# Layernorm, linear attention and a Mish feed-forward on one core: statistics by tile, the first weight matrix in three loads, the opening products on a constant, a new order of steps

## The chip, the core and the metric

The kernel runs on one core of a Trainium2 chip. The core has five engines with queues of their own: PE (TensorE, matrix products), ACT (ScalarE), DVE (VectorE), POOL (GpSimd) and SP (SyncE, which here only issues DMA transfers). Each engine takes its instructions strictly in the order in which they were written, and waits on semaphores for the other engines. The metric is the device time of one execution in microseconds; lower is better.

## What is computed

The reference, cut to what matters (`S` = 2048 rows, `D` = 448, 16 heads of 28, `F` = 1792; everything in bf16):

```python
def reference(A_x, A_wqkv, A_w_phi, A_wo, B_x, B_w1, B_b1, B_w2):
    xn = layernorm(A_x)                       # over the last axis, eps 1e-5
    q, k, v = split_heads(xn @ A_wqkv)
    pq, pk = q @ A_w_phi[h], k @ A_w_phi[h]   # per head, 28 x 28
    phi_q = concat(softmax(pq), softmax(-pq)) # 56 features
    phi_k = concat(softmax(pk), softmax(-pk))
    kv, z = phi_k.T @ v, phi_k.sum(rows)      # no causal mask
    o = (phi_q @ kv) / (phi_q @ z + 1e-6)
    h = xn @ B_w1 + B_b1
    act = h * tanh(softplus(h))               # Mish
    return A_x + o @ A_wo + act @ B_w2
```

## The kernel before

The 2048 rows are 16 tiles `t` of 128 rows, taken in 8 pairs `u`. All of it stays in SBUF. The steps are functions, each with a short name, and one long string `ORDER` (L147) lists the names in the order in which the functions are called (`run_order`, L163). Each function appends its operations to the queue of the engine that does them, so `ORDER` sets the order on every engine at once; `resolve` (L89) puts in the waits. A letter behind a name picks the engine: `a` for ACT, `d` for DVE, `p` for POOL, `m` or `s` for a transfer by SP, `b` for both ACT and DVE.

The stages, with the names that matter below:

- `z12` (`warm`, L366) puts 12 products of 128x128 by 128x512 ahead of everything on PE. Their operands are one element of a bf16 tile `zeros` that POOL clears (`zero`, L313), repeated by a stride of 0; nobody reads what they write.
- `lx0s` to `lx6s` load the rows of x, `lkms`, `lkts`, `lvms` the k and v parts of the qkv weights, `lqT0` to `lqT3` the q part transposed, `l1ms` and `l1ts` the matrix W1 (rows 0 to 383 in one load, the last 64 rows twice), `l2s` W2, `los` the output weights. All are issued by SP.
- `st` computes mean and variance of a pair (on DVE, or with `b` one of the two tiles on ACT), `rs` the power -1/2 of the variance (ACT: Ln and Exp; POOL: an add and a power), `xn` the normalised rows, `xt` their transposes (on PE with a copy out by ACT or DVE, or by a DMA transpose).
- `wtk`, `wmk`, `wmq` fold the 28x28 feature weights into the k and q weights (transposes and small products on PE, copies on ACT and DVE).
- `k`, `q`, `v` with a pair number are the projections of a pair, `f0.` and `f1.` the products with W1 for one of 14 column blocks and one half of the rows. Each has two parts: `F` is the three full chunks of 128 in the contraction (6 products), `H` the last 64 rows (2 products). The part that comes second closes the pair of PSUM banks and is followed by the copy out: two exponentials on ACT for k and q, one copy for v, one Mish activation on ACT for f.
- `kn` normalises phi_k (a sum and a reciprocal on DVE, a product on POOL), `kv` sums phi_k.T v on PE, `kvz` copies it out and has it transposed by DMA. `e` is the DMA transpose of phi_q of one tile. `nd` is the numerator and denominator of one tile on PE and the division on DVE, `ot` the DMA transpose of the result.
- `wo` and `g` (14 products a tile) are the products with the output weights and W2 into the same banks; `sto` and `stt` store. For the last tile, 15, the last 64 columns are computed apart (`last_columns`, L788).

A step that reads W1 waits for all of its loads, since `rows_of("W1")` (L287) lists them all, whichever rows the step needs.

Of the kernel before, what the change touches and what calls it, by code (L numbers as in the profile page):

```python
# [12 lines left out]
D = 448  # L13
# [3 lines left out]
P = 128  # L17
# [132 lines left out]
st4 k2F rs4p wmq0d xn4d xn5p wmq1a k3F v1Fd st0 q3F k1H q3H lx6s st6 v1Hd q2H q2F rs6p st7 k1F q1F rs0p xt4m xt5m  # L150
xn6d k4F rs7p k4H e6 v5Hd xn0d xt6m xn7d kn4.1 q1H k5H xt0m v5Fd k5F kn5.0 v6Fd kn5.1 k6F k0H xt7m ep e7 v6Ha k7H
l1ts l1ms k6H k7F kn6.0 k0F kn6.1 e3 q6F e2 v0Fa kn2.1 kn7.1 v4Fd v0Ha v4Hd kn4.0 q6H v7Hd kn3.0 v7Fa q4F e4 e12
f1.2H q4H e9 f0.2H kn2.0 e13 f0.2F kn7.0 f0.0F f1.2F f0.1F f0.0H f0.1H f1.3H q5H kn1.0 f1.3F kn0.1 e8 q0F q0H f0.3H
kn0.0 q7H kn3.1 e5 e1 q5F q7F f0.3F f1.7F kv7 kn1.1 kv0 kv4 kv6 kv3 kv2 kv1 e0 kv5 e10 f1.1H kvz f1.7H f1.8H f1.1F
f1.8F f0.6F e14 e11 f1.5H f0.6H nd2 f0.10F f1.5F nd1 f0.10H f0.5H f0.5F f1.11F nd3 ot1m f1.11H nd0 f0.13H f0.13F e15
f1.12F f1.0F f1.0H ot0m f1.12H los wob nd6 f1.13F f0.7F f1.10H f0.7H nd7 l2s ot3m f1.13H f1.10F f0.4F f0.4H nd5
f0.12H f0.9H f0.9F f0.12F nd4 f0.11H f0.8H f0.8F f0.11F f1.4F f1.6H f1.4H nd10 ot2m f1.9H f1.9F f1.6F wo3F wo3H nd11
nd13 nd12 ot5m ot6m g7 g6 g10 g11 wo5H nd15 nd14 wo2H wo5F ot7m g5 sto3 g4 wo2F wo6F sto5 wo6H wo1H nd9 nd8 wo1F sto2
g12 g2 g14 g13 wo7F wo0F ot4m wo0H sto6 wo4H wo7H g3 g0 wo4F g1 g8 stt14 sto0 g9 sto1 sto4 g15 stt15
"""  # L160
# [7 lines left out]
def _kernel(es, nc, A_x, A_wqkv, A_w_phi, A_wo, B_w1, B_b1, B_w2, out):  # L168
    def sb(name, shape, dtype):
        return es.enter_context(nc.sbuf_tensor(name, shape, dtype))  # L170
# [61 lines left out]
    def Eq_of(u):  # L232
        if u % 3 == 0:
# [5 lines left out]
                 "Wp1": [("Wp", 1, h, c) for h in range(2) for c in range(2)]}  # L239

    def oT_of(u):
# [6 lines left out]
    def bank(b, n=1):  # L248
        return PS[:, b * TCW:(b + n) * TCW]
# [61 lines left out]


    def p_zero():  # L313
        op("POOL", lambda e: e.memset(zeros[:], 0.0), w=[("zeros",)], tag="zeros")

# [50 lines left out]
    def warm(n):  # L366
        b = take1()

        def f(e):
            for _ in range(n):  # L370
                ins = e.matmul(bank(b)[:, :], ap_on(zeros[:, 0:1], [[0, P]]), ap_on(zeros[:, 0:1], [[0, TCW]]), start=True,
                               stop=True)
            return ins
        pe(f, [("zeros",)], [pb(b)], f"warm{n}")

# [66 lines left out]

    def ln_stats(u, both=False):
        for t in (2 * u, 2 * u + 1):
            if both and t % 2:
                i = u % 2
                op("ACT", lambda e, t=t: e.activation(junk[i][:], x_all[:, t, :], ACT.Copy, scale=1.0 / D,
                                                      accum_out=mv[:, t, 0:1]),
                   r=[("x", t), ("junk", i)], w=[("mean", t), ("junk", i)], tag=f"sm{t}")
                op("ACT", lambda e, t=t: e.mul(rmean[:, i:i + 1], mv[:, t, 0:1], D ** -0.5), r=[("mean", t)],  # L450
                   w=[("rmean", i)], tag=f"rm{t}")
                op("ACT", lambda e, t=t: e.activation(junk[i][:], x_all[:, t, :], ACT.Square, bias=rmean[:, i:i + 1],
                                                      scale=-D ** -0.5, accum_out=mv[:, t, 1:2]),
                   r=[("x", t), ("rmean", i), ("junk", i)], w=[("mv", t), ("junk", i)], tag=f"sq{t}")
                continue
            op("DVE", lambda e, t=t: e.bn_stats(stats[:, t, :], x_all[:, t, :]), r=[("x", t)], w=[("st", t)],  # L456
               tag=f"bn{t}")
            op("DVE", lambda e, t=t: e.bn_aggr(mv[:, t, :], stats[:, t, :]), r=[("st", t)], w=[("mv", t), ("mean", t)],
               tag=f"ag{t}")

    def ln_rstd(u, eng):
        a, b = 2 * u, 2 * u + 2
        if eng == "POOL":
            op("POOL", lambda e: e.tensor_scalar(lnv[:, a:b], mv[:, a:b, 1], float(LN_EPS), 0.0, op0=ALU.add,
                                                 op1=ALU.add),
               r=[("mv", a), ("mv", a + 1)], w=[("lnv", u)], tag=f"vare{u}")
            op("POOL", lambda e: e.tensor_tensor(rstd[:, a:b], lnv[:, a:b], mhalf[:], ALU.pow),
               r=[("lnv", u), ("eps",)], w=[("rstd", u)], tag=f"rstd{u}")
            return
        op("ACT", lambda e: e.activation(lnv[:, a:b], mv[:, a:b, 1], ACT.Ln, bias=eps_col[:]),  # L470
           r=[("eps",), ("table",), ("mv", a), ("mv", a + 1)], w=[("lnv", u)], tag=f"ln{u}")
        op("ACT", lambda e: e.activation(rstd[:, a:b], lnv[:, a:b], ACT.Exp, scale=-0.5),
           r=[("lnv", u)], w=[("rstd", u)], tag=f"rstd{u}")

    def ln_pair(u, eng):
        X = xn[u % NXN]
        a, b = 2 * u, 2 * u + 2
        if eng == "POOL":
            op("DVE", lambda e: e.scalar_tensor_tensor(shift[:, a:b], mv[:, a:b, 0], -1.0, rstd[:, a:b], ALU.mult,
                                                       ALU.mult),  # L480
               r=[("mean", a), ("mean", a + 1), ("rstd", u)], w=[("sh", u)], tag=f"sh{u}")
        for t in (a, a + 1):
            parts = [(0, D, 0)] if t % 2 == 0 else [(384, D, D), (0, 384, D + 64)]
            for n, (lo, hi, at) in enumerate(parts):
                if eng == "POOL":
                    op("POOL", lambda e, t=t, lo=lo, hi=hi, at=at: e.tensor_scalar(
                        X[:, at:at + hi - lo], x_all[:, t, lo:hi], rstd[:, t:t + 1], shift[:, t:t + 1],
                        op0=ALU.mult, op1=ALU.add),
                       r=[("x", t), ("sh", u), ("rstd", u)], w=[("xn", u % NXN, t % 2, n)], tag=f"xn{t}.{n}")
                else:  # L490
                    op("DVE", lambda e, t=t, lo=lo, hi=hi, at=at: e.tensor_scalar(
                        X[:, at:at + hi - lo], x_all[:, t, lo:hi], mv[:, t, 0:1], rstd[:, t:t + 1],
                        op0=ALU.subtract, op1=ALU.mult),
                       r=[("x", t), ("mean", t), ("rstd", u)], w=[("xn", u % NXN, t % 2, n)], tag=f"xn{t}.{n}")

# [358 lines left out]
    for u in range(NU):  # L854
        add(f"st{u}", ln_stats, u)
        add(f"st{u}b", ln_stats, u, True)
        add(f"xt{u}b", xT, u, "both")
        for eng, c in (("ACT", "a"), ("POOL", "p")):
            add(f"rs{u}{c}", ln_rstd, u, eng)
# [34 lines left out]
    for eng, c in (("SP", "s"), ("ACT", "a")):  # L894
# [13 lines left out]
    add("qd", double_qT)  # L908
    for n, fn in (("pi", p_ident), ("pm", p_mask), ("pw", p_wbd), ("pv", p_ones), ("pk", p_mask2), ("pp", p_pads), ("zero", p_zero)):
        add(n, fn)  # L910
    for n in (1, 2, 4, 8, 12):
        add(f"z{n}", warm, n)
# [53 lines left out]
```

## Time and profile before

| | us |
|---|---|
| median of 3 runs | 156.11 (155.65 to 156.21) |
| span of the profiled execution, first to last instruction | 152.5 |
| busy: PE, DVE, ACT, POOL | 147.9, 101.2, 74.9, 39.9 |
| the 12 opening products on PE | 0.95 to 6.25 |
| first product on real data | 6.70 |

The profile follows one execution. It lists its span, 152.5 us, and no time of the whole of it, so the span stands beside the median of the other runs, 3.6 us below it; that difference lies ahead of the first instruction and behind the last. A row of the timeline has the start in us from the span's start, the time from the first start to the last end, the engine, the line of the kernel, the operation with out<-in, the tile it works on, and how many instructions are merged in the row. In square brackets stands the idle time ahead of it and what ended it. `PEld` is the weight load of a product, which overlaps with the product ahead of it. A product's row contains the time until its result has landed; products in a row start closer together than their durations say.

### The profile page before, as it was taken

Reading aid. Unit: us, or ns where it says so; the run is one execution under the profiler, and the core shown is the slowest. Engines: PE = TensorE matmul, PEld = TensorE weight load, DVE = VectorE, ACT = ScalarE, POOL = GpSimd, SP = SyncE. Lnnn points to the kernel's source line nnn. Section 1 sums busy time; section 2 is a strip of 40 time slices with the busy share of each in tenths; the row PEclk is TensorE's granted clock in tenths of the full one; section 3 lists DMA queues with packets and bytes.
Section 4 is the critical chain, followed back from the end, with each engine's and each line's share of the span. In section 5 each row is a group of like instructions: output and inputs, shape, how many; then the busy total and the mean of one; then the engine's idle time right before and its main releaser. Section 6 shows DMA issues by size and latency. Waiting matters only on the chain.

```text
span 152.5 us, 2888 instructions
## 1 busy us (share of the span) xinstructions
PE 147.9 (97%) x1181; PEld 72.7 (48%) x1181; DVE 101.2 (66%) x227; ACT 74.9 (49%) x91; POOL 39.9 (26%) x58
## 2 busy tenths in 40 slices
PE   7899999999998999999999999999999999999993
PEld 2365444454443466444444444555555555455552
DVE  1699997999999203198999847798695970311221
ACT  4888899898599996757459657100000000000000
POOL 7452552499999950000000000000000000000000
PEclk9999999999999999999999999999999999999999
DMA  5995576889969176830379941030206111110302
GB/s 130 274 238 97 175 136 127 177 236 257 189 141 192 24 160 55 135 71 0 64 149 302 338 75 25 4 62 6 54 0 195 50 34 26 60 34 0 120 0 90
DMA packets 39961, 17.17 MB, mean 113 GB/s; under 512 B 33932, under 2 KB 39180, under 8 KB 39948
## 3 DMA queue, kind: packets, MB, share of 16 engines
q1 hardware_dynamic: 39804, 16.89, 49.2%
q8 instruction: 9, 0.15, 0.4%
q10 hardware_dynamic: 144, 0.10, 0.2%
q14 instruction: 4, 0.03, 0.1%
HBM read 7.02 MB, written 1.84 MB: 58 GB/s over the span
## 4 chain that ended last, share of the span: by engine, by line
PE 82%; DMA 7%; ACT 6%; SPq 2%; DVE 0%; issue 0%; ACTq 0%
PE PS L426 40%; PE PS L816 28%; PE PS L832 7%; DMA EqT<-actT 4%; DMA Wkv<-in_A_wqkv_dram 3%; PE PS L716 3%; PE PS L642 2%; ACT actT L613 2%; ACT actT L693 1%; ACT actT L674 1%; PE PS L575 1%; ACT L693 1%; ACT v_all L504 1%; SPq L268 1%; SPq L682 1%; PE PS L551 0%
## 5 line engine op out<-in xcount | busy, mean ns | idle before, releaser
L426 PE MATMUL PS<-xnT,W 128*128 128x512 bf16 (+1 forms) x224 | 46.3, 379 | 0.0
L816 PE MATMUL PS<-W,actT 128*128 128x448 bf16 (+1 forms) x224 | 42.8, 351 | 0.0
L693 ACT ACTIVATE actT<-PS,b1T 128x1024 bf16<-128x1024 f32 x28 | 30.3, 1114 | 13.1 <-PE PS L426 13.0
L816 PEld LDWEIGHTS PS<-W,actT 128*128 128x128 bf16 x224 | 21.8, 98 | 20.2 <-issue 0.4
L426 PEld LDWEIGHTS PS<-xnT,W 128*128 128x128 bf16 (+1 forms) x224 | 17.6, 97 | 23.7 <-issue 5.1
L625 POOL TENSOR_TENSOR actT<-actT,rSk 128x896 bf16<-128x896 bf16 x16 | 26.6, 1701 | 4.4 <-DVE rSk L623 4.4
L781 DVE TENSOR_TENSOR x_all<-PS,x_all 128x448 bf16<-128x448 f32 (+1 forms) x16 | 9.6, 617 | 20.9 <-PE PS L816 17.7
L621 DVE TENSOR_REDUCE Sk<-actT 128x32 f32<-128x896 bf16 x16 | 16.7, 1042 | 0.9 <-ACT actT L613 0.9
L613 ACT ACTIVATE actT<-PS 128x896 bf16<-128x896 f32 x16 | 13.7, 940 | 0.4 <-PE PS L426 0.4
L426 PE MATMUL PS<-Wpq,xnT 128*128 128x448 bf16 (+1 forms) x64 | 12.9, 353 | 0.5 <-ACT actT L693 0.5
L426 PE MATMUL PS<-Wpk,xnT 128*128 128x448 bf16 (+1 forms) x64 | 12.7, 353 | 0.0
L426 PE MATMUL PS<-Wkv,xnT 128*128 128x448 bf16 (+1 forms) x64 | 12.6, 353 | 0.0
L731 DVE COPY Sq<-PS 128x16 f32<-128x16 f32 x32 | 4.0, 167 | 10.8 <-PE PS L716 10.8
L456 DVE BATCH_NORM_STATS2 stats<-x_all 128x6 f32<-128x448 bf16 x14 | 8.5, 605 | 3.4 <-DMA x_all<-in_A_x_dram 3.4
L739 DVE TENSOR_TENSOR v_all<-v_all 128x464 f32<-128x464 f32 x16 | 10.3, 642 | 0.6
L735 DVE TENSOR_TENSOR v_all<-PS,Sq 128x464 f32<-128x464 f32 x16 | 10.3, 641 | 0.5
L742 DVE TENSOR_TENSOR xn<-v_all,rden 128x448 bf16<-128x448 f32 x16 | 10.0, 625 | 0.6
L737 DVE TENSOR_TENSOR v_all<-PS,Sq 128x464 f32<-128x464 f32 x16 | 10.1, 629 | 0.0
L674 ACT ACTIVATE actT<-PS 128x896 bf16<-128x896 f32 x10 | 8.5, 932 | 1.7 <-DMA EqT<-actT 1.7
L426 PEld LDWEIGHTS PS<-Wpq,xnT 128*128 128x128 bf16 (+1 forms) x64 | 5.3, 97 | 6.5 <-issue 1.1
L426 PEld LDWEIGHTS PS<-Wpk,xnT 128*128 128x128 bf16 (+1 forms) x64 | 5.3, 97 | 6.1 <-issue 1.9
L426 PEld LDWEIGHTS PS<-Wkv,xnT 128*128 128x128 bf16 (+1 forms) x64 | 5.0, 97 | 5.7 <-issue 1.5
(86 smaller groups left out, 118.0 us busy)
## 6 DMA issues: line engine op xcount, KB each, us to landing
W<-in_B_w_dram SPq DMA_DIRECT2D x1, 1568.0 KB, 7.8
out_dram<-x_all SPq DMA_DIRECT2D x7, 224.0 KB, 2.2
W<-in_B_w_dram SPq DMA_DIRECT2D x1, 1344.0 KB, 9.0
x_all<-in_A_x_dram SPq DMA_DIRECT2D x4, 224.0 KB, 3.2
x_all<-in_A_x_dram SPq DMA_DIRECT2D x2, 448.0 KB, 4.6
Wkv<-in_A_wqkv_dram SPq DMA_DIRECT2D x2, 336.0 KB, 4.5
Wo<-in_A_wo_dram SPq DMA_DIRECT2D x2, 336.0 KB, 3.9
W<-in_B_w_dram SPq DMA_DIRECT2D x2, 224.0 KB, 3.6
```

What stands on the lines that cost most here:

```text
L426: ins = e.matmul(o, lhs(c, k), rhs(c, k), start=first and c in (0, 3), stop=not first and c in (2, 3))
L613: op("ACT", lambda e, s=s: e.activation(E_of(u)[:, s, :, :], two(b, D), ACT.Exp, scale=1.0 if s == 0 else -1.0), r=[pb(b), pb(b + 1)], w=[ ...
L621: op("DVE", lambda e: e.tensor_reduce(Sk[u][:, s, :], Eh(), AX.X, ALU.add), r=[("E", u, s)], w=[("Sk", u, s)], tag=f"Sk{u}.{s}")
L625: op("POOL", lambda e: e.tensor_tensor(Eh(), Eh(), ap_on(rSk[u][:, s, 0:1], [[1, 2 * H], [0, DH]]), ALU.mult), r=[("E", u, s), ("rSk", u, ...
L674: op("ACT", lambda e, s=s: e.activation(Eq_of(u)[:, :, s, :].rearrange("p i (h n) -> p i h n", n=64)[:, :, :, 0:QP], two(b, D).rearrange(" ...
L693: op("ACT", lambda e: e.activation(actT[:, fc, q * 1024:(q + 1) * 1024], bank(b, 2), ACT.Mish, bias=b1T[:, fc:fc + 1]), r=[("b1T",), pb(b) ...
L735: op("DVE", lambda e: e.tensor_tensor(tv(t1[i]), num(0), sx(1), ALU.mult), r=[pb(b), pb(b + 1), ("Sq", i, 1)], w=[("t1", i)], tag=f"ta{t}")
L737: op("DVE", lambda e: e.tensor_tensor(tv(t2), num(1), sx(0), ALU.mult), r=[pb(b), pb(b + 1), ("Sq", i, 0)], w=[("t2",)], tag=f"tb{t}")
L739: op("DVE", lambda e: e.tensor_tensor(t1[i], t1[i], t2, ALU.add), r=[("t1", i), ("t2",)], w=[("t1", i)], tag=f"tc{t}")
L742: op("DVE", lambda e: e.tensor_tensor(o_sb[(t // 2) % 2][:, t % 2, :].rearrange("p (h d) -> p h d", d=DH), t1[i][:, :, 0:DH], ap_on(rden[i ...
L816: ins = e.matmul(bank(b)[:, 0:width(t)], actT[:, fc, tok(t)], W2[:, fc, 0:width(t)], start=first and fc == 0, stop=last and fc == FC - 1)
L832: ins = e.matmul(bank(b)[:, 0:n], oT_of(u)[lo:hi, cc * P:(cc + 1) * P], Wo[lo:hi, cc, 0:n], start=first and c in (0, 3), stop=last and c i ...
```

## The change

Four things are changed.

1. `zeros` and the step that clears it are gone. `warm` reads one element of a constant 1.0 that the framework keeps in SBUF, and waits for nothing. The constant that `scalar_like` gives is the float32 one, so the products are of float32 operands; there are 10 of them (`z10`) in place of 12. In the compiled program a float32 product is two pairs of weight load and matmul, so PE's queue begins with 20 such pairs; a bf16 product is one.
2. `st` and the waits on powers go by tile: `st3d` is tile 3 on DVE, `st2a` tile 2 on ACT, and `rs1t` does Ln and Exp of each of the two tiles by itself.
3. W1's 384 rows are loaded in three parts (`l1m0s`, `l1m1s`, `l1m2s`), each at a place of its own; a step that reads W1 waits for all three and for the last rows.
4. All steps stand in a new order. Among others the pairs 1 and 3 of x come first in place of 2 and 3, and ffn products with W2 (`g`) begin while products with W1 still run. The home of a transposed output is claimed by whichever pair comes first (`homes_taken`).

The order on PE at the program's beginning, where the opening products stand; before:

```order
L371 MATMUL PS<-zeros 128x512 [waits done_POOL]
L371 MATMUL PS<-zeros 128x512 x11
L551 MATMUL PS<-ident,Wkv 112x128 [waits dma_2,done_POOL]
L551 MATMUL PS<-ident,Wkv 112x128 x7
L499 MATMUL PS<-ident,xn 128x128 [waits done_DVE]
L499 MATMUL PS<-ident,xn 128x128 x6
```

and now:

```order
L376 MATMUL PS<-const-float32-1.0 128x512 x10
L552 MATMUL PS<-ident,Wkv 112x128 [waits dma_2,done_POOL]
L552 MATMUL PS<-ident,Wkv 112x128 x7
L500 MATMUL PS<-ident,xn 128x128 [waits done_DVE]
L500 MATMUL PS<-ident,xn 128x128 x6
```

The wait for POOL ahead of the first product is gone, the operand is the float32 constant, and the first product on real data follows the tenth, waiting for the same load of the k weights (`dma_2`) as before.

SP's queue around the loads of W1 (`W`) and the transposes of phi_q (`EqT`); before:

```order
L511 DMA_TRANSPOSE xnT<-xn 128x7x128 [waits done_DVE] x3
L682 DMA_TRANSPOSE EqT<-Eq 128x8x128
L276 DMA W<-in_B_w_dram 64x1792 x2
L271 DMA W<-in_B_w_dram 128x3x1792
L682 DMA_TRANSPOSE EqT<-actT 128x8x128 [waits done_ACT]
L682 DMA_TRANSPOSE EqT<-actT 128x8x128 x2
L682 DMA_TRANSPOSE EqT<-Eq 128x8x128 [waits done_ACT]
```

and now:

```order
L281 DMA W<-in_B_w_dram 64x1792 x2
L277 DMA W<-in_B_w_dram 128x1792
L512 DMA_TRANSPOSE xnT<-xn 128x7x128 [waits done_DVE] x3
L683 DMA_TRANSPOSE EqT<-actT 128x8x128 [waits done_ACT]
L683 DMA_TRANSPOSE EqT<-actT 128x8x128
L683 DMA_TRANSPOSE EqT<-actT 128x8x128 [waits done_ACT]
L683 DMA_TRANSPOSE EqT<-Eq 128x8x128 [waits done_ACT]
L277 DMA W<-in_B_w_dram 128x1792
L512 DMA_TRANSPOSE xnT<-xn 128x7x128 [waits done_POOL]
L683 DMA_TRANSPOSE EqT<-Eq 128x8x128
L277 DMA W<-in_B_w_dram 128x1792
```

The one large load ahead of the next transposes of phi_q has become three smaller ones, the second behind four of these transposes and the third behind a fifth; a transpose of x (of pair 0, normalised by POOL) now stands between the two transposes of phi_q of pair 3.

The end of SP's queue; before:

```order
L846 DMA out_dram<-x_all 128x448 [waits done_DVE]
L846 DMA out_dram<-x_all 128x896 [waits done_DVE]
L846 DMA out_dram<-x_all 128x896
L846 DMA out_dram<-x_all 128x896 [waits done_DVE]
L843 DMA out_dram<-x_all 128x64 [waits done_DVE]
```

and now:

```order
L848 DMA out_dram<-x_all 128x448 [waits done_DVE]
L848 DMA out_dram<-x_all 128x896 [waits done_DVE] x2
L848 DMA out_dram<-x_all 128x896 x2
L845 DMA out_dram<-x_all 128x64 [waits done_DVE]
```

Four stores of pairs stand behind that of tile 14 in place of three.

The diff, cut to its core:

```diff
 ORDER = """
-table lx2s zero lx3s pv st2b pw lkms lps pi pm st3b rs3a lkts z12 pp lbs rs2p lx1s xn2d xn3d wtk0b xt2b wtk1b lvms
-lx4s lqT2 st1 bd pk lqT0 xt3a b1 wmk0b lqT1 rs1a wmk1a xn1d st5 rs5p v2Fd lqT3 v3Fa v3Ha k2H v2Ha k3H qd xt1m lx0s
...
+pv lx1s st3d table pi pw st2a lx3s z10 lkms st6d lps lkts lbs lvms st7d rs1t pp xn1d lx2s rs3a lqT0 xn3d wtk0a xt1d
+wtk1b lx0s pm xt3b bd wmk0a wmk1a st4d v3Fd st5d lx6s v1Ha lqT1 rs2t lqT2 xn2d v3Ha b1 st15d st14d lqT3 qd xt2m k3H
+lx4s k3F v1Fa k1F wmq1a st0d rs7p st12d wmq0a xn7p xt7m l1ts st1d l1m1s st13d pk rs6p st11d k2F k2H k1H st8d st9d v2Ha
+q1H st10d q1F xn6d rs0p v2Fd q2F q3F k7H rs4p rs5p xt6m q2H q3H xn4d xn5d kn2.1 v7Ha xt4m v7Fd kn3.0 k7F xn0p v6Fa
+xt5m e2 k4F k4H k6H e3 e5 v6Hd q4H k6F e7 l1m2s q4F kn7.1 kn6.1 v5Fd v4Fd q6H xt0m k5H v5Hd e6 l1m0s k5F kn4.1 q6F
...
+f1.5H nd13 g2 f1.4F f1.7H f1.4H sto0 ot6m nd10 f1.7F f1.9F wo1F g6 f1.9H ot5m f1.12H nd14 wo3H f1.12F wo3F g7 wo5F nd9
+wo5H nd15 nd8 g10 ot7m g8 g12 wo6F sto1 g11 g5 g9 wo7F ot4m g4 wo6H wo4H wo7H wo2H g14 sto5 wo2F stt14 g13 wo4F sto6
+sto4 sto2 g15 sto3 stt15
 """
...
-    zeros = sb("zeros", [P, 2], BF16)
...
+    def load_chunk(eng, name, dst, src, c):
+        dma(eng, lambda e: e.dma_start(dst[:, c, :], src[c * P:(c + 1) * P, :]), w=[(name, 0, c)], tag=f"ld{name}.{c}")
...
-        return [(name, 0), ("Wt", 0), ("Wt", 1)] if name in ("Wk", "Wv") else [(name, i) for i in range(3)]
+        if name in ("Wk", "Wv"):
+            return [(name, 0), ("Wt", 0), ("Wt", 1)]
+        return [("W1", 0, c) for c in range(3)] + [("W1", 1), ("W1", 2)]
...
-    def p_zero():
-        op("POOL", lambda e: e.memset(zeros[:], 0.0), w=[("zeros",)], tag="zeros")
...
     def warm(n):
         b = take1()
+        one = nc.const_aps.scalar_like(1.0, ident[:, 0:1])
 
         def f(e):
             for _ in range(n):
-                ins = e.matmul(bank(b)[:, :], ap_on(zeros[:, 0:1], [[0, P]]), ap_on(zeros[:, 0:1], [[0, TCW]]), start=True,
-                               stop=True)
+                ins = e.matmul(bank(b)[:, :], ap_on(one, [[0, P]]), ap_on(one, [[0, TCW]]), start=True, stop=True)
             return ins
-        pe(f, [("zeros",)], [pb(b)], f"warm{n}")
+        pe(f, [], [pb(b)], f"warm{n}")
...
-    def ln_stats(u, both=False):
-        for t in (2 * u, 2 * u + 1):
-            if both and t % 2:
...
+    def ln_stats(t, eng):
+        if eng == "ACT":
...
+        for n, m in ((a, b),) if eng == "ACT" else ((a, a + 1), (a + 1, b)):
+            op("ACT", lambda e, n=n, m=m: e.activation(lnv[:, n:m], mv[:, n:m, 1], ACT.Ln, bias=eps_col[:]),
+               r=[("eps",), ("table",)] + [("mv", t) for t in range(n, m)], w=[("lnv", t) for t in range(n, m)], tag=f"ln{n}")
+            op("ACT", lambda e, n=n, m=m: e.activation(rstd[:, n:m], lnv[:, n:m], ACT.Exp, scale=-0.5),
+               r=[("lnv", t) for t in range(n, m)], w=[("rstd", t) for t in range(n, m)], tag=f"rstd{n}")
...
-        home = [("oT", u)] + ([x for n in oT_home[u // 2][2] for x in home_rows[n]] if u % 2 == 0 else [])
+        home = [("oT", u)] + ([x for n in oT_home[u // 2][2] for x in home_rows[n]] if u // 2 not in homes_taken else [])
+        homes_taken.add(u // 2)
...
-        add(f"l1m{c}", load_main, eng, "W1", W1, B_w1)
+        for i in range(3):
+            add(f"l1m{i}{c}", load_chunk, eng, "W1", W1, B_w1, i)
...
-    for n in (1, 2, 4, 8, 12):
+    for n in (4, 8, 10, 12, 14):
         add(f"z{n}", warm, n)
```

More of the change, by code (lines that the diff above doesn't have):

```diff
@@ L153 @@
[L153 to L157, printed above, removed]
@@ L439, in step @@
         return add
[L443 to L459 removed]
+    def ln_stats(t, eng):
+        if eng == "ACT":
+            i = t // 2 % 2
+            op("ACT", lambda e: e.activation(junk[i][:], x_all[:, t, :], ACT.Copy, scale=1.0 / D, accum_out=mv[:, t, 0:1]),
+               r=[("x", t), ("junk", i)], w=[("mean", t), ("junk", i)], tag=f"sm{t}")
+            op("ACT", lambda e: e.mul(rmean[:, i:i + 1], mv[:, t, 0:1], D ** -0.5), r=[("mean", t)], w=[("rmean", i)],
+               tag=f"rm{t}")
+            op("ACT", lambda e: e.activation(junk[i][:], x_all[:, t, :], ACT.Square, bias=rmean[:, i:i + 1],
+                                             scale=-D ** -0.5, accum_out=mv[:, t, 1:2]),
+               r=[("x", t), ("rmean", i), ("junk", i)], w=[("mv", t), ("junk", i)], tag=f"sq{t}")
+            return
+        op("DVE", lambda e: e.bn_stats(stats[:, t, :], x_all[:, t, :]), r=[("x", t)], w=[("st", t)], tag=f"bn{t}")
+        op("DVE", lambda e: e.bn_aggr(mv[:, t, :], stats[:, t, :]), r=[("st", t)], w=[("mv", t), ("mean", t)], tag=f"ag{t}")
     def ln_rstd(u, eng):
@@ L465, in ln_rstd @@
                                                  op1=ALU.add),
-               r=[("mv", a), ("mv", a + 1)], w=[("lnv", u)], tag=f"vare{u}")
+               r=[("mv", a), ("mv", a + 1)], w=[("lnv", a), ("lnv", a + 1)], tag=f"vare{u}")
             op("POOL", lambda e: e.tensor_tensor(rstd[:, a:b], lnv[:, a:b], mhalf[:], ALU.pow),
-               r=[("lnv", u), ("eps",)], w=[("rstd", u)], tag=f"rstd{u}")
+               r=[("lnv", a), ("lnv", a + 1), ("eps",)], w=[("rstd", a), ("rstd", a + 1)], tag=f"rstd{u}")
             return
[L470 to L473, printed above, removed]
+        for n, m in ((a, b),) if eng == "ACT" else ((a, a + 1), (a + 1, b)):
[3 more added lines that the diff above has]
+               r=[("lnv", t) for t in range(n, m)], w=[("rstd", t) for t in range(n, m)], tag=f"rstd{n}")
     def ln_pair(u, eng):
@@ L854, in _kernel @@
     for u in range(NU):
-        add(f"st{u}", ln_stats, u)
-        add(f"st{u}b", ln_stats, u, True)
+        for t in (2 * u, 2 * u + 1):
+            for eng, c in (("DVE", "d"), ("ACT", "a")):
+                add(f"st{t}{c}", ln_stats, t, eng)
         add(f"xt{u}b", xT, u, "both")
-        for eng, c in (("ACT", "a"), ("POOL", "p")):
+        for eng, c in (("ACT", "a"), ("POOL", "p"), ("tiles", "t")):
             add(f"rs{u}{c}", ln_rstd, u, eng)
@@ L908, in _kernel @@
     add("qd", double_qT)
-    for n, fn in (("pi", p_ident), ("pm", p_mask), ("pw", p_wbd), ("pv", p_ones), ("pk", p_mask2), ("pp", p_pads), ("zero", p_zero)):
+    for n, fn in (("pi", p_ident), ("pm", p_mask), ("pw", p_wbd), ("pv", p_ones), ("pk", p_mask2), ("pp", p_pads)):
         add(n, fn)
-    for n in (1, 2, 4, 8, 12):
+    for n in (4, 8, 10, 12, 14):
         add(f"z{n}", warm, n)
```

17 lines of the change are left out of this document (9 added, 8 removed).

## Prediction

> **What bounds the kernel now.** I read the page's busy times first, then PE's waits, then PE in order of time, then the chain of waits.
>
> ```profile
> span 152.5 us, 2888 instructions
> PE 147.9 (97%) x1181; PEld 72.7 (48%) x1181; DVE 101.2 (66%) x227; ACT 74.9 (49%) x91; POOL 39.9 (26%) x58
> PE PS L371 <- POOL zeros L314: 1.0, 1, 1.0
> PE PS L551 <- DMA Wkv<-in_A_wqkv_dram: 0.7, 2, 0.4
> PE PS L426 <- ACT actT L693: 0.5, 1, 0.5
> ```
>
> PE is busy for 97% of the span, and its waits are three lines that add up to 2.2 us. In order of time they lie here:
>
> ```profile
> 0.95 5.30 PE L371 MATMUL PS<-zeros 128*128 128x512 bf16 x12 [0.95 <-POOL zeros L314]
> 6.70 0.63 PE L551 MATMUL PS<-ident,Wkv 128*112 128x128 bf16 x8 [0.45 <-DMA Wkv<-in_A_wqkv_dram]
> ...
> 7.97 0.65 PE L551 MATMUL PS<-ident,Wkv 128*112 128x128 bf16 x8 [0.23 <-DMA Wkv<-in_A_wqkv_dram]
> ...
> 46.90 0.36 PE L426 MATMUL PS<-Wpq,xnT 64*128 64x448 bf16 x2 [0.46 <-ACT actT L693]
> ...
> 149.45 0.57 PE L798 MATMUL PS<-W,actT 128*128 128x64 bf16 x14
> ```
>
> So the span is a sum over PE. Its opening products, which nobody reads, are busy from 0.95 to 6.25. Real work starts at 6.70, when the k weights have landed, and the last product ends at 150.02. Of the 147.9 us busy, 147.9 - 5.3 = 142.6 are real work; inside it PE idles 0.23 + 0.46 = 0.69, and 152.5 - 150.0 = 2.5 follow it. Whatever moves the start of real work moves the end, and nothing else has much to give: all idle time on PE between real work's start and its end is worth 0.69 us.
>
> **The change part by part.** The opening products first, since they stand ahead of everything on PE. PE's queue is in order, so the first product on real data cannot start before the tenth of them is done. Their start moves a little: the constants are written ahead of the kernel's own first steps, and the wait for `zeros` goes.
>
> ```profile
> 0.34 0.10 POOL L951 MEMSET const-float32-1.0<- 128x1 f32 x1
> ...
> 0.80 0.10 POOL L314 MEMSET zeros<- 128x2 bf16 x1 [0.29 <-POOLq L951]
> ```
>
> The other engines begin at 0.80, so I let PE begin there, 0.15 earlier. Then the price. Before, 12 products of bf16:
>
> ```profile
> L371 PE MATMUL PS<-zeros x12: 610/634/634, 1.0 to 5.6; 128*128 128x512 bf16 x12
> 52.71 2.75 PE L426 MATMUL PS<-xnT,W 128*128 128x512 bf16 x12
> PEclk9999999999999999999999999999999999999999
> ```
>
> The first row (durations least/median/most, first and last start) gives one start every (5.65 - 0.95)/11 = 0.427 us, and the second 2.75/12 = 0.23 us for products of the same width later on. PE starts slow, although the clock's row on the page, the third, shows full speed in every slice, and it is still slow in the twelfth product, at 5.65. The products of 128 columns at 6.70 are fast (8 in 0.63). I put the rise at 6.2.
>
> Now there are 10 products of float32, compiled to 20 pairs of weight load and product, each reading 4 bytes an element. No row of PE here has a 4-byte operand. The nearest rows are copies out of PSUM by other engines:
>
> ```profile
> 8.33 0.41 DVE L506 COPY Eq<-PS 112x512 bf16<-112x512 bf16 x1
> 10.85 0.62 DVE L506 CAST Wpk<-PS 128x448 bf16<-128x448 f32 x1
> 7.43 0.60 ACT L504 ACTIVATE Eq<-PS 112x512 bf16<-112x512 bf16 x1 [0.19 <-PE PS L551]
> 9.96 0.55 ACT L504 ACTIVATE Wpk<-PS 128x448 bf16<-128x448 f32 x1
> ```
>
> Per element a 4-byte source costs DVE (0.62/448)/(0.41/512) = 1.73 times a 2-byte one, and ACT (0.55/448)/(0.60/512) = 1.05 times. So a pair costs between once the bf16 row and twice it (twice the bytes). With the rise at 6.2, that is 5.4 us after the start:
>
> - once: 5.4/0.427 = 12.6 pairs slow, 7.4 at 0.23 = 1.7; real work starts at 0.8 + 5.4 + 1.7 = 7.9
> - 1.73 times: 5.4/0.739 = 7.3 slow, 12.7 at 0.40 = 5.1; at 11.3
> - twice: 5.4/0.854 = 6.3 slow, 13.7 at 0.46 = 6.3; at 12.5
> - twice and never fast: 20 at 0.854 = 17.1; at 17.9
>
> I take 1.73, from the engine that is nearer to a bound by bytes, inside the two ends. The cover is the wait for the k weights, which hides products up to 6.67 and no more; with real work at 11.3 some 4.6 us lie open.
>
> The Trainium skill, "FP8 and Floating Point Precision", section "TensorE Precision Notes", says that true FP32 takes four passes through the array. By it a product would cost 4 x 0.427 = 1.71 us slow and 0.92 fast, which is the line "twice"; no row here shows it.
>
> The statistics. One tile less goes through ACT and one more through DVE, and `rs1t` adds an Ln and an Exp of one column:
>
> ```profile
> 6.70 0.29 ACT L470 ACTIVATE lnv<-mv,eps_col 128x2 f32<-128x2 f32 x1
> 7.03 0.20 ACT L472 ACTIVATE rstd<-lnv 128x2 f32<-128x2 f32 x1
> ```
>
> That is 0.5 us on ACT, all ahead of 11.3 and under the opening products: 0. If the products were short, it would delay the first transposes by up to 0.5.
>
> W1 in three loads and the new order. The stall at 46.90 is the one thing that they can mend. The chain of waits tells where it comes from:
>
> ```profile
> 34.38 0.78 SPq L682
> ...
> 35.20 6.42 DMA EqT<-actT
> ACT actT L674 <- DMA EqT<-actT: 1.7, 1, 1.7
> EqT<-actT SPq DMA_TRANSPOSE x10, 3.3
> W<-in_B_w_dram SPq DMA_DIRECT2D x1, 1344.0 KB, 9.0
> ```
>
> A transpose of phi_q took 6.42 us where the median is 3.3, in the 9.0 us in which W1's large load was landing; ACT waited for it before it could overwrite phi_q's buffer, and PE ran out of PSUM banks 5 us later. With a third of the load at a time I expect this stall to go, -0.46, and the 0.23 at 7.97 too, since the tails of the weights have long landed by 11.3. But the new order brings a chain of its own. In SP's queue the second transpose of pair 3 stands behind a transpose of x that waits for POOL, and ACT's exponentials of pair 6 wait for it; and the operations on ACT leave little room:
>
> ```profile
> 20.61 1.30 PE L426 MATMUL PS<-Wpk,xnT 128*128 128x448 bf16 x6
> 21.74 1.30 PE L426 MATMUL PS<-Wpq,xnT 128*128 128x448 bf16 x6
> 19.25 1.73 ACT L674 ACTIVATE Eq<-PS 128x896 bf16<-128x896 f32 x2 [0.59 <-PE PS L426]
> ```
>
> A pair's k or q costs PE 1.13 for the full chunks and 0.19 for the rest, 1.32, against 1.73 on ACT. Summed in the written order, ACT's work is at most 0.5 us ahead of PE's before and 0.6 now, so four pairs of banks hold it as before. Two of v's copies move from ACT to DVE, which is busy for 66% of the span and waits for PE after them as it did. Bounds for stalls of the new order: 0 and 1.5, a transpose that lands 2.7 late of which ACT's slack takes 1.2 (before, ACT's 1.7 of waiting became 0.46 on PE). I take 0.3.
>
> The end. Four stores stand behind tile 14's in place of three, the last three behind tiles 8 and 9, some 1.0 us ahead of the end of the last products.
>
> ```profile
> 149.53 0.56 DVE x_all L781
> ...
> 150.31 0.33 SPq L843 DMA_DIRECT2D out_dram<-x_all  x1
> out_dram<-x_all SPq DMA_DIRECT2D x7, 224.0 KB, 2.2
> out_dram<-x_all SPq DMA_DIRECT2D x1, 16.0 KB, 1.7
> ```
>
> Three issues of about 0.5 end about when the last DVE operation does, and a store of 224 KB lands only 0.5 later than one of 16 KB, so the last small store is not held up: 0, at most +0.5.
>
> The sum for the span: 11.3 + 142.6 + 0.3 + 2.5 = 156.7, against 152.5, that is +4.2. The median of the runs is 3.6 above the profiled span; I carry that over: 160.3 us.
>
> **The rivals.** *The clock does not rise while the opening products run.* The trace shows it rise under bf16 products only; whether 4-byte ones, with pauses between columns, count for as much is not in it. At 1.73 they end at 0.8 + 20 x 0.739 = 15.6, at twice at 17.9, and real work then starts slow and, if it needs the same 5.4 us, loses half of them, 2.7. Span 15.6 + 2.7 + 142.6 + 0.3 + 2.5 = 163.7, or 166.0: 167.3 to 169.6 us. For it speaks that PE was slow for all of 5 us before; against it, that it was busy throughout, as it would be now. The Trainium skill, "TensorE: Matmul & The Clock Gate", Part 1, has the clock follow how busy PE was in a window of about 3.4 us that runs free; by that it rises under any products, the rise may fall earlier or later from one execution to the next, and the row agrees in so far as twelve starts from 0.95 to 5.65 were all slow.
>
> *The opening products cost little: the other side.* If each pair costs what a bf16 product does, real work starts at 7.9, and with both inner stalls gone and none of the new order the span is 7.9 + 142.6 + 2.5 = 153.0: 156.6 us, not slower by what can be told. The point from which it decides is real work's start at 7.4 (152.5 - 142.6 - 2.5), ten products in 6.6 us together: below it the change gains. At most it gains down to the wait for the k weights: 6.7 + 142.6 + 2.5 = 151.8, 155.4 us. For it: ACT's 1.05. Against it: twenty instructions in place of twelve, and twice the bytes.
>
> *The new order stalls on pair 3's transpose*, on top of the forecast: 3.2 late, 1.2 of it absorbed, 2.0 on PE: 162.0 us. For it: ACT has waited for just such a transfer. Against it: with PE 4.6 later, everything that does not hang on PE (loads, statistics, the transposes of x) is that much earlier beside it.
>
> *The change does not do what its words say.* That is so in one point: the constant is neither zero nor 2 bytes wide; the forecast is made of that. If the chip runs each of them as one bf16 product all the same, ten take 4.3, end by 5.1, and real work waits for the k weights at 6.70 as before: 6.7 + 142.6 + 0.3 + 2.5 = 152.1, 155.7 us.
>
> **How the numbers follow.** Forecast (rise during the products, a price between 1.4 and 2 times): 0.55. Clock not risen: 0.22. Stalls of the new order on top: 0.11. Little cost: 0.08. One pass: 0.04. The forecast's own range is 158.5 to 162.5: the line "twice" gives 12.5 + 142.6 + 0.3 + 2.5 + 3.6 = 161.5, and 1.4 times (9.0 pairs slow at 0.598, 11.0 at 0.32, real work at 9.7) gives 158.7. For 8 in 10 I take the forecast, the stalls and the half of the slow clock that lies at 1.73, and leave out the other side but for its edge: 157.5 to 168.5. A difference below 0.5%, 0.78 us, can't be told from none here. The last two cases lie between 155.4 and 156.6, mostly within 0.5%: 0.07 same, 0.03 faster, and 0.02 of them above, which joins the rest: slower 0.90.
>
> **What would show it.** The row of the opening products: 10 or 20 float32 products that end near 11 (right), by 7 (hidden), or beyond 15 with the first 128-column products of real work at half pace (clock). Real work's first row then starts without idle time ahead of it, in place of 0.45 on the k weights. PE's waits inside real work should add up to less than 0.7, without a line of ACT's Mish. The chain should run over PE from about 0.8 on. The forecast is wrong if real work starts before 8, if PE has more than 1.5 us of waits behind it, or if the span from PE's last product to the end grows beyond 3.

## The result, and the profile after

The changed kernel takes 159.52 us (median of 4 runs, 158.98 to 160.56) against 155.88 for the kernel before in the same runs: a ratio of 1.028, interval 1.020 to 1.036. The profiled execution took 159.65 us with a span of 157.9. Run once more in a later job the ratio was 1.032 (1.027 to 1.037), where 2.0 to 3.6% was expected. The forecast was 160.3. The kernel before took 154.5 to 154.6 us in the later jobs (medians of 17 to 23 runs), so its 155.88 here, a median of four, is on the long side and the ratio of 1.028 on the low one.

The page of the kernel after, its span, busy times and the row of the opening products (engine, operation, tile, count, then busy time, mean ns of one, idle time ahead):

```profile
span 157.9 us, 2913 instructions
PE 153.3 (97%) x1189; PEld 75.8 (48%) x1189; DVE 102.9 (65%) x226; ACT 73.6 (47%) x91; POOL 40.6 (26%) x58
L376 PE MATMUL PS<-const-float32-1.0 128*128 128x512 f32 x20 | 10.9, 708 | 0.8 <-PEq L955 0.8
```

PE is again busy for 97%, and the twenty float32 products make 10.9 us of that where twelve bf16 ones made 5.3. Without them PE's work is 153.3 - 10.9 = 142.4, as before (142.6). PE in order of time, every row with idle time ahead of it, and the first real products:

```profile
0.84 10.91 PE L376 MATMUL PS<-const-float32-1.0 128*128 128x512 f32 x20 [0.84 <-PEq L955]
11.58 0.61 PE L552 MATMUL PS<-ident,Wkv 128*112 128x128 bf16 x8
...
14.33 1.78 PE L430 MATMUL PS<-Wkv,xnT 128*128 128x448 bf16 x10
...
31.03 1.30 PE L430 MATMUL PS<-Wkv,xnT 128*128 128x448 bf16 x6 [0.32 <-DMA xnT<-xn]
32.75 1.78 PE L430 MATMUL PS<-Wpk,xnT 128*128 128x448 bf16 x10 [0.43 <-DMA xnT<-xn]
...
70.84 0.40 PE L717 MATMUL PS<-KVZ,EqT 56*128 56x60 bf16 x16 [0.36 <-DMA KVZ<-KVT]
...
154.73 0.57 PE L800 MATMUL PS<-W,actT 128*128 128x64 bf16 x14
```

Real work starts at 11.58 with no idle time ahead of it, 4.88 later than before. The two waits inside real work (0.23 on weights, 0.46 behind a Mish) are gone, and three others have come, 1.11 us together, all on DMA transposes: two of x (pairs 6 and 4), one of the summed phi_k v. The last product ends at 155.30 and 2.6 us follow. So the span grew by 4.88 at the start, 1.11 - 0.69 = 0.4 in the middle and 0.1 at the end, 5.4 in all.

How a float32 product is paid is read from its weight loads (start, duration, idle ahead):

```profile
3.53 0.34 PEld L376 LDWEIGHTS PS<-const-float32-1.0 128*128 128x128 f32 x1 [0.52 <-issue]
4.39 0.34 PEld L376 LDWEIGHTS PS<-const-float32-1.0 128*128 128x128 f32 x1 [0.52 <-issue]
5.12 0.19 PEld L376 LDWEIGHTS PS<-const-float32-1.0 128*128 128x128 f32 x1 [0.39 <-issue]
5.55 0.19 PEld L376 LDWEIGHTS PS<-const-float32-1.0 128*128 128x128 f32 x1 [0.24 <-issue]
5.98 0.19 PEld L376 LDWEIGHTS PS<-const-float32-1.0 128*128 128x128 f32 x1 [0.24 <-issue]
```

A pair of load and product takes 0.86 us at first and 0.43 from about 5.0 on: at the slow pace twice the 0.427 of a bf16 product, and at the fast pace about twice the 0.22 to 0.23 that bf16 products of this width take. The pace rose during these products.

### The profile page after: what moved, and what is told of

It reads as the page before. It is cut to its first block, busy times and chain, and to the rows that moved or that the text cites. A ratio compares the mean times of both kernels' runs of the same rounds, so it can differ in the third digit from the quotient of the medians.

```text
span 157.9 us, 2913 instructions
## 1 busy us (share of the span) xinstructions
PE 153.3 (97%) x1189; PEld 75.8 (48%) x1189; DVE 102.9 (65%) x226; ACT 73.6 (47%) x91; POOL 40.6 (26%) x58
## 4 chain that ended last, share of the span: by engine, by line
PE 81%; DMA 8%; DVE 4%; POOL 2%; ACT 2%; issue 1%; SPq 0%; DVEq 0%; ACTq 0%
PE PS L430 35%; PE PS L818 27%; PE PS L376 7%; PE PS L834 7%; DMA xnT<-xn 3%; DMA KVZ<-KVT 3%; PE PS L717 2%; DMA x_all<-in_A_x_dram 2%; PE PS L643 2%; POOL rstd L467 2%; DVE stats L458 1%; ACT Eq L505 1%; DVE KVT L655 1%; ACT Wpk L505 1%; DVE xn L492 1%
## 5 line engine op out<-in xcount | busy, mean ns | idle before, releaser
L430 PE MATMUL PS<-xnT,W 128*128 128x512 bf16 (+1 forms) x224 | 46.8, 379 | 0.0
L818 PE MATMUL PS<-W,actT 128*128 128x448 bf16 (+1 forms) x224 | 44.0, 351 | 0.0
L376 PE MATMUL PS<-const-float32-1.0 128*128 128x512 f32 x20 | 10.9, 708 | 0.8 <-PEq L955 0.8
L458 DVE BATCH_NORM_STATS2 stats<-x_all 128x6 f32<-128x448 bf16 x15 | 9.1, 605 | 3.6 <-DMA x_all<-in_A_x_dram 3.6
```

The lines of the kernel that those rows point to most:

```text
L376: ins = e.matmul(bank(b)[:, :], ap_on(one, [[0, P]]), ap_on(one, [[0, TCW]]), start=True, stop=True)
L430: ins = e.matmul(o, lhs(c, k), rhs(c, k), start=first and c in (0, 3), stop=not first and c in (2, 3))
L458: op("DVE", lambda e: e.bn_stats(stats[:, t, :], x_all[:, t, :]), r=[("x", t)], w=[("st", t)], tag=f"bn{t}")
L818: ins = e.matmul(bank(b)[:, 0:width(t)], actT[:, fc, tok(t)], W2[:, fc, 0:width(t)], start=first and fc == 0, stop=last and fc == FC - 1)
```

## Experiments

Each ratio is against the kernel before, run in the same job, with its 95% interval; its median there was 154.5 to 154.6 us.

| run | what it is | us | ratio |
|---|---|---|---|
| new_order_bf16 | changed kernel, ten bf16 opening products | 157.78 | 1.021 (1.018 to 1.024) |
| old_order_f32 | kernel before, ten float32 opening products | 158.63 | 1.026 (1.023 to 1.030) |
| old_order_bf16 | kernel before, twelve bf16 ones, constant 1.0 | 154.86 | 1.003 (1.000 to 1.006) |
| new_w1_whole | changed kernel, W1's rows in one load | 165.29 | 1.070 (1.065 to 1.076) |
| new_bf16_14 | changed kernel, fourteen bf16 opening products | 156.46 | 1.014 (1.011 to 1.017) |
| new_bf16_14_w1_late | the same, two loads of W1 later | 155.56 | 1.008 (1.005 to 1.012) |
| old_w1_three | kernel before, W1 in three loads | 153.92 | 0.996 (0.995 to 0.998) |
| old_bf16_10 | kernel before, ten bf16 opening products | 156.16 | 1.010 (1.005 to 1.015) |
| new_f32_6 | changed kernel, six float32 products | 158.05 | 1.023 (1.019 to 1.027) |
| changed_again | the changed kernel | 159.49 | 1.032 (1.027 to 1.037) |
| old_w1_three_14 | old_w1_three, fourteen opening products | 154.15 | 0.997 (0.995 to 1.000) |
| old_w1_three_b | old_w1_three, loads at other places | 155.53 | 1.007 (1.004 to 1.009) |

### The opening products undone, and alone

new_order_bf16:

```diff
-        one = nc.const_aps.scalar_like(1.0, ident[:, 0:1])
+        one = nc.const_aps.scalar_like(1.0, ident[:, 0:1], BF16)
```

> The changed kernel with one thing undone: the opening ten products read a bf16 constant 1.0 in place of the float32 one. Theory A (the opening products make the loss): they end near 5.1, real work starts at the landing of the k weights, 6.7, in place of 11.6, so the time falls by up to 4.9 us from 159.5, to 154.6; up to 1 us less if stalls that the late start hid come out, such as the waits for the transposes of x (0.75 us on PE in the changed kernel). Theory B (the new order makes the loss): real work starts at 6.7 but PE's waits grow by what was gained, and the time stays within 1 us of 159.5.

old_order_f32 (the kernel before with `warm` of the changed one, and `z10`):

```diff
+        one = nc.const_aps.scalar_like(1.0, ident[:, 0:1])
...
-                ins = e.matmul(bank(b)[:, :], ap_on(zeros[:, 0:1], [[0, P]]), ap_on(zeros[:, 0:1], [[0, TCW]]), start=True,
-                               stop=True)
+                ins = e.matmul(bank(b)[:, :], ap_on(one, [[0, P]]), ap_on(one, [[0, TCW]]), start=True, stop=True)
...
-        pe(f, [("zeros",)], [pb(b)], f"warm{n}")
+        pe(f, [], [pb(b)], f"warm{n}")
```

> The kernel before with the opening products alone changed: ten products on the float32 constant in place of twelve on zeros. Theory A: real work starts at 11.6 in place of 6.7, both waits of 0.45 and 0.23 on weights are gone, and the time rises by 4.2 to 4.9 us over the kernel before. Theory B: it rises by less than 1 us.

In the old order the float32 products cost 4.1 us (158.63 against 154.5) by themselves: theory A, just under its 4.2 to 4.9, with real work at 11.48 in that profile. But in the new order taking them away gave back only 1.7: 157.78, still 2.1% over the kernel before. That lies between the two theories. PE of new_order_bf16, its rows with idle time ahead and the first real products:

```profile
0.84 4.42 PE L376 MATMUL PS<-const-bfloat16-1.0 128*128 128x512 bf16 x10 [0.84 <-PEq L955]
6.71 1.07 PE L552 MATMUL PS<-ident,Wkv 128*112 128x128 bf16 x8 [1.45 <-DMA Wkv<-in_A_wqkv_dram]
7.58 0.95 PE L500 MATMUL PS<-ident,xn 128*128 128x128 bf16 x7
...
10.83 1.78 PE L430 MATMUL PS<-Wkv,xnT 128*128 128x448 bf16 x10
...
17.91 1.78 PE L430 MATMUL PS<-Wpk,xnT 128*128 128x448 bf16 x10 [0.59 <-DMA xnT<-xn]
28.10 1.30 PE L430 MATMUL PS<-Wkv,xnT 128*128 128x448 bf16 x6 [0.15 <-DMA xnT<-xn]
40.44 1.29 PE L430 MATMUL PS<-Wkv,xnT 128*128 128x448 bf16 x6 [1.35 <-DMA xnT<-xn]
69.20 0.40 PE L717 MATMUL PS<-KVZ,EqT 56*128 56x60 bf16 x16 [0.74 <-DMA KVZ<-KVT]
```

Real work does start at 6.71, 4.87 earlier. Then two things take it back. Eight products of 128 columns take 1.07 us where they took 0.61: PE runs at half pace there, and its first long products come at 10.83, 4.1 after real work's start where the changed kernel needs 2.75 (11.58 to 14.33). That is 1.4. And the waits for transposes are 2.83 where the late start left 1.11. 4.87 - 1.4 - 1.7 = 1.8, and the span fell by 157.9 - 156.2 = 1.7.

old_order_bf16 is the same edit as old_order_f32 with the bf16 constant and twelve products.

> The kernel before with its twelve opening products on the bf16 constant 1.0: no wait for the cleared tile, nothing else. Theory A: they start 0.15 earlier and end before the k weights land, real work starts at 6.7 as before, and the time is the same within 0.5 us. A rival: products of ones in place of zeros, or an earlier start, raise PE's pace at another moment; then the first real products are slow or fast and the time moves by up to 1.5 us.

Together the wait for the cleared tile and the value of the constant are worth nothing that can be told from none (0.3%, 0.0 to 0.6%).

### Half pace at the start of real work

new_bf16_14 has `z14` in place of `z10` in new_order_bf16; old_bf16_10 has `z10` in place of `z12` in old_order_bf16.

> The changed kernel with fourteen bf16 opening products in place of ten float32 ones. Theory A (after ten bf16 products PE was idle for 1.45 us and real work began at half pace, which cost 1.4 us): fourteen end near 6.8, just as the k weights land, the first 128-column products take 0.6 us for eight in place of 1.07, and the time falls by 1.0 to 1.4 us below the run with ten bf16 products, to 3.3 - 1.2 = about 2 us over the kernel before. Rival: the pace at real work's start hangs on the moment at which the execution began, not on these products; then nothing changes.

> The kernel before with ten bf16 opening products on the constant in place of twelve on zeros. Theory A (too few products leave PE at half pace when real work starts, whatever the order): real work starts at half pace and the time rises by 1.0 to 1.5 us over the kernel before. Rival: in the old order the pace at the start does not matter, because copies and loads bound the first 3 us of real work; the time is the same within 0.4 us.

Both times moved about as theory A said: four more products in the new order save 1.3 us (156.46 against 157.78), two fewer in the old one cost 1.3 (156.16 against 154.86), or 1.6 over the kernel before. Both pairs of medians join two jobs, in which the kernel before differed by 0.1. The four runs of old_bf16_10 lie between 154.69 and 156.65, one of them at the time of the kernel before; so the rival, by which the moment of an execution also counts, is not ruled out. In new_bf16_14 the products last until real work, which runs at full pace:

```profile
0.84 5.91 PE L376 MATMUL PS<-const-bfloat16-1.0 128*128 128x512 bf16 x14 [0.84 <-PEq L955]
6.94 0.63 PE L552 MATMUL PS<-ident,Wkv 128*112 128x128 bf16 x8 [0.19 <-DMA Wkv<-in_A_wqkv_dram]
```

The profile of old_bf16_10 shows another course:

```profile
0.84 4.04 PE L372 MATMUL PS<-const-bfloat16-1.0 128*128 128x512 bf16 x10 [0.84 <-PEq L951]
7.09 0.62 PE L551 MATMUL PS<-ident,Wkv 128*112 128x128 bf16 x8 [2.21 <-DMA Wkv<-in_A_wqkv_dram]
7.56 0.75 PE L499 MATMUL PS<-ident,xn 128*128 128x128 bf16 x7
8.10 1.06 PE L551 MATMUL PS<-ident,Wkv 128*112 128x128 bf16 x8
8.95 0.95 PE L499 MATMUL PS<-ident,xn 128*128 128x128 bf16 x7
```

Eight products run at full pace after 2.21 us of idle time, the pace falls within the next seven, and from 8.10 on it is half. So real work did not start at half pace, as theory A had it; the pace was lost a little later. In new_order_bf16 it had not risen at all: its ten opening products lie 0.43 us apart from the first to the last, and the first real ones run on at half pace. Nor does the length of the idle time alone decide. In old_w1_three, a run of the next section with twelve opening products, it is as long as in new_order_bf16, and real work starts at full pace and keeps it:

```profile
0.95 5.07 PE L376 MATMUL PS<-zeros 128*128 128x512 bf16 x12 [0.95 <-POOL zeros L319]
7.46 0.62 PE L556 MATMUL PS<-ident,Wkv 128*112 128x128 bf16 x8 [1.44 <-DMA Wkv<-in_A_wqkv_dram]
```

More opening products helped here, and in new_bf16_14 fourteen cost nothing, since they end before the k weights land. By which rule the pace rises and falls these runs do not settle.

### W1 in three loads, in both orders

new_w1_whole has `l1ms` (one load) where the changed kernel has `l1m1s`, and neither of the two others.

> The changed kernel with W1's 384 rows in one load again, at the place of the first of the three loads. Theory A: with real work at 11.6 and the next transposes of phi_q behind the whole load, one of them lands some 3 us late as before, of which ACT's slack takes most: 159.5 to 160.5 us. A rival: W1 in three loads is worth more than that, and the time rises by 1 to 2 us.

A miss for both: 165.29 us, some 6 us over the changed kernel (159.5 in other jobs). Its chain of waits (start, duration, what) and PE around it:

```profile
26.99 9.55 DMA xnT<-xn
36.53 0.14 issue
...
36.67 2.40 PE L430 MATMUL PS<-Wkv,xnT 128*128 128x448 bf16 x6 [5.38 <-DMA xnT<-xn]
```

I had looked at the transposes of phi_q and not at the three of x that stand directly behind the load in SP's queue. One of them lands after 9.55 us, PE idles 5.38 and then runs six products in 2.40 where they take 1.30 at full pace. In the new order the three loads are no gain but a need: a whole load just ahead of a transpose that PE waits for costs far more than a third of it does.

new_bf16_14_w1_late asks the same of the 1.35 us at 40.44 in new_order_bf16, whose chain reads

```profile
33.40 0.58 SPq L277
34.03 6.27 DMA xnT<-xn
```

a third of W1 issued at 33.40, and right behind it the transpose of pair 0 that takes 6.27 us. The edit moves that load:

```diff
-... e7 l1m2s q4F ... xt0m k5H v5Hd e6 l1m0s ...
+... e7 q4F ... xt0m k5H v5Hd e6 l1m2s l1m0s ...
```

> The same with fourteen bf16 products, and the second and third load of W1's rows behind the transpose of x of pair 0 and the last transpose of phi_q of pair 3, not around them. Theory A (transposes on SP's queue land late because a load of W1 was issued just ahead): the wait of 1.35 us on PE for the transpose of pair 0 goes, and the time falls by 1.0 to 1.4 us below the run with fourteen alone, to about 1 us over the kernel before. Rival (POOL's normalising of pair 0 is what is late): the wait stays above 0.9 us and the time is the same.

The wait for that transpose is gone, and the time fell by 0.9 us, a little less than expected; the seven runs lie between 155.08 and 156.52, the longest as long as those with fourteen alone. What is left of PE's waits in this kernel:

```profile
PE PS L552 <- DMA Wkv<-in_A_wqkv_dram: 1.3, 2, 1.2
PE PS L376 <- PEq L955: 0.8, 1, 0.8
PE PS L430 <- DMA xnT<-xn: 0.6, 1, 0.6
PE PS L717 <- DMA KVZ<-KVT: 0.4, 1, 0.4
```

0.6 + 0.4 are on transposes. That is near the 0.96 us by which this kernel still stands over the kernel before, but the kernel before has 0.69 of waits of its own behind real work's start, so the two do not account for the whole. What does wasn't tried.

The old order with three loads, old_w1_three (`load_chunk` and `rows_of` as in the change):

```diff
-... wmk1a xn1d st5 ... lx6s st6 v1Hd ... v6Ha k7H l1ts l1ms k6H ...
+... wmk1a xn1d st5 ... lx6s l1ts l1m0s st6 v1Hd ... v6Ha k7H l1m1s l1m2s k6H ...
```

> The kernel before with W1 in three loads alone: its last rows and the first third are issued behind the last loads of x, some 14 us earlier, and the other two thirds where the whole load stood. Theory A: the transpose of phi_q that took 6.4 us behind the whole load takes 3 less, PE's wait of 0.46 for a pair of banks goes, and the time falls by 0.3 to 0.5 us, if the early third does not delay the transposes of x issued behind it. Rival: they are delayed, PE waits for a transpose of x as in the changed kernel with W1 whole (5.4 us there for a whole load, so 2 us for a third and the last rows), and the time rises by 0.5 to 2 us.

0.7 us faster: this edit, and its variant with fourteen products below, are the only ones that beat the kernel before by more than their intervals. Its profile has no wait behind a Mish any more and a new one of 0.73 us for a transpose of x, so both sides of the expectation are in it. But the profiled execution, 155.44 us, is not a typical one: 11 of the 13 runs took 153.52 to 154.21. The profile of old_w1_three_14, 153.87 us in the same order, has neither wait. Two variants did not get further. old_w1_three_14 has `z14`, old_w1_three_b has `l1m0s` behind `e6` in place of ahead of the transposes of pairs 4 and 5.

> The old order with W1 in three loads and fourteen opening products on the bf16 zeros in place of twelve. Theory A: fourteen end at 6.9 at the latest, about when the k weights land, so nothing is delayed by more than 0.2 and PE's pace cannot fall in the idle time before real work; the median stays within 0.3 us of the same with twelve and the spread upwards shrinks (no run over 155.5). Rival: they delay real work by up to 0.5 and the time rises by as much.

> The old order with W1 in three loads, the last rows early and the first third behind the transpose of phi_q of tile 6, not ahead of the transposes of x of pairs 4 and 5. Theory A (transposes land late behind a load that was issued just ahead): PE's wait of 0.73 us for a transpose of x in the run before this one goes or shrinks below 0.3, and the time is 0.3 to 0.7 us below that run, 0.5 to 0.9% under the kernel before. Rival: the wait moves to the transposes issued next, and the time is the same.

Fourteen products change nothing that can be told from twelve, and the longest run is 155.01 in place of 156.02. The other places made it worse: the wait for a transpose of x is 2.29 us at 29.93, since the third now stands ahead of three other transposes. The rival was right that the wait moves, and wrong that the time would be the same. The expectation was built on the wait of 0.73 in a long execution, which the typical ones may not have.

### Fewer float32 products

new_f32_6 has `z6` in the changed kernel.

> The changed kernel with six float32 opening products in place of ten. Theory A (each is two pairs, 0.85 us a pair slow and 0.43 fast, and real work cannot start before the last): 12 pairs, about 5 slow and 7 fast, are 7.3 us, real work starts near 8.2, 3.4 us earlier than with ten; the stalls of the new order that the late start hid come out in part (about 1 us), so the time falls by 2 to 3 us below the changed kernel in this job. Rival (the pace while they run hangs on their count): all 12 slow, 10.2 us, real work at 11.1, and the time falls by less than 1 us.

```profile
0.84 7.27 PE L376 MATMUL PS<-const-float32-1.0 128*128 128x512 f32 x12 [0.84 <-PEq L955]
7.95 0.61 PE L552 MATMUL PS<-ident,Wkv 128*112 128x128 bf16 x8
...
17.96 1.78 PE L430 MATMUL PS<-Wpk,xnT 128*128 128x448 bf16 x10 [0.78 <-ACT Wpq L505]
39.81 1.29 PE L430 MATMUL PS<-Wkv,xnT 128*128 128x448 bf16 x6 [0.95 <-DMA xnT<-xn]
68.90 0.40 PE L717 MATMUL PS<-KVZ,EqT 56*128 56x60 bf16 x16 [1.06 <-ACT actT L694]
```

The price by pairs holds (7.3 expected, 7.27 measured; real work at 7.95 for 8.2). But of the 3.6 us by which real work starts earlier than at 11.58 only 1.4 reach the end by the medians (158.05 against 159.49 in the same job) and 2.0 by the two spans (155.9 against 157.9), at or under the low edge of the 2 to 3 expected: PE's waits in real work are 2.8 us in place of 1.1.

## Why the prediction was right, point by point

**The start of real work** was put at 11.3 and measured at 11.58. Two errors cancelled in it, so that it came so near is luck. The price of a pair was taken as 1.73 times a bf16 product, by analogy with DVE's copies, and is 2.0 times at the slow pace and 1.9 at the fast; the rise of the pace was put at 6.2 and came at about 5.0. With twice the price and the rise at 6.2 the prediction's own line gave 12.5. The Trainium skill, "FP8 and Floating Point Precision", section "TensorE Precision Notes", gives four passes for true FP32: two pairs of twice a bf16 product are four, 1.70 us slow and 0.86 fast, and the trace agrees. In the old order this price alone, with no other change, costs 4.1 us.

**The clock** did rise under float32 products, so the rival that it would not is out. When it rises differs between executions: fourteen bf16 products took 5.91 us in one profile and 4.76 in another. By the Trainium skill, "TensorE: Matmul & The Clock Gate", Part 1, the window in which the activity is measured runs free of the program; those two rows agree. The changed kernel's own two profiles differ likewise: real work starts at 11.58 in one and at 12.07 in the other (changed_again).

**The stalls of the new order** were mis-sized and misplaced. The term was 0.3 us, and the place a transpose of phi_q of pair 3 that delays ACT. Measured were 1.11 us in the changed kernel, at transposes of x and of the summed phi_k v on PE itself. The step that failed is the belief that with real work later everything off PE is early. The chain of waits of the changed kernel to the wait at 32.75 shows it (start, duration, what):

```profile
12.29 1.51 ACT Eq L505 x2
...
17.95 0.66 SPq L512
...
18.65 3.63 DMA x_all<-in_A_x_dram
...
22.30 0.64 DVE stats L458
...
28.36 4.25 DMA xnT<-xn
```

ACT's first copy waits for the first real products of PE, further copies and the powers of pair 2 follow it, and only then can pair 2 be normalised and its transpose issued. A load of x (`lx4s`) stands behind that transpose in SP's queue, so it too is late, and with it the statistics, the powers on POOL and the transpose of pair 4. So the late start of PE moves this chain along, and only part of it is bought off. Two of the prediction's signs failed here: PE's waits were to stay under 0.7, and the chain was to run over PE from 0.8 on, where it leaves PE from 12.2 to 32.75.

**The sum's last term was wrong and hid that.** I carried the 3.6 us between the profiled span of before and the median of its runs over to the change, and wrote that they lie ahead of the first instruction and behind the last. In every later profile, where both times are of one execution, the rest around the span is 1.7 to 2.0 (159.65 - 157.9 = 1.75), so the profiled execution of before took about 154.2 to 154.5, less than the three runs shown with it. The forecast span was 1.2 too short (156.7 against 157.9) and this term 1.9 too long; 160.3 against 159.5 is the difference, with the runs' own scatter. That the forecast came within 0.8 us is thus in part luck; the mechanism, products on PE that real work must wait for, is as forecast.

**The rival with little cost** is out, since its condition was not met, and what it drew from the condition fails as well. It said that with cheap opening products the kernel would not be slower. With ten bf16 ones it is 2.1% slower, with fourteen 1.4%: the new order, with the loads and statistics that belong to it, has a price of its own. It is not the whole 3.3 us of new_order_bf16, since the old order with ten bf16 products pays 1.6 too: 1.6 us is left (157.78 - 156.16), and with fourteen 1.9 (156.46 - 154.6, against twelve in the kernel before). Alone the float32 products cost 4.1 us. Both together cost 4.9 (159.49 - 154.59; 3.6 in the first job, 159.52 - 155.88), which is 0.8 more, so about half of the new order's price lies under the late start.

**The stall of 0.46 behind a Mish** went, as forecast; in the old order three loads alone are worth 0.4% (0.2 to 0.5%) all told. **The statistics by tile** were put at nothing because their powers lie under the opening products. Those of pairs 1 and 3 do, they end near 6.5; those of pair 2 also go by tile (`rs2t`), run from 15.7 to 16.6 and stand on the chain shown above. What they cost no run isolates. **The end** was right: 2.6 us behind the last product for 2.5, with four stores queued there.

## What to carry to other kernels

Work that nobody reads is still work when it stands first in an in-order queue: count its instructions in the compiled program and look at the type of its operands before calling it free. A late start hides stalls behind it, so undoing it returns less than it cost, and a new order is to be judged with the start repaired. Ahead of a DMA transpose that the busiest engine waits for, count the bytes issued on the same queue just before it, and compare each profile's span with the time of its own execution.

## What was not expected of the hardware

- PE's pace fell to half after 2.21 us without products, not at once but more than eight products later, and stayed there until about 11.3 (old_bf16_10; its granted clock reads 0.50 from 8 to 11 us). In new_order_bf16 the granted clock reads 1.00 from 7 to 10 us at the same half pace, and in the pages of both kernels the clock's row shows full speed where the opening products run at half pace. So the pace is better read from the distance between starts.
- Transposes issued behind a load of weights land late: one of x after 9.55 us behind a whole load and the last rows, one after 6.27 behind a third, where the median of a transpose of x before was 3.1. The delay does not go with the bytes alone: in the kernel before a transpose of phi_q took 6.42 behind the whole load.
